# Routed attention and a bilinear FFN on one core: pair numbers instead of counts, closer issues, two more probability rooms

## The chip, the cores and the metric

The kernel runs on one core of one Trainium2 chip. The metric is the device time of one execution in microseconds (us); the table below gives the runs of the kernel before. The profile is of one further execution, recorded with its engines: TensorE (PE, with its weight loads PEld), VectorE (DVE), ScalarE (ACT), GpSimd (POOL) and SyncE (SP), which issues most DMAs.

## What is computed

Queries and keys of each head are assigned to the nearest of 16 centroids; a query attends to the keys of its own cluster alone. The heads' outputs, side by side, are the input of a feed-forward network with two factors. The shapes are (4, 8, 768, 64) for q, k and v, (8, 16, 64) for the centroids, (512, 1536) twice and (1536, 512) for the weights.

```python
q_assign = argmax(q_n @ c_n.T); k_assign = argmax(k_n @ c_n.T)
mask = q_assign[:, :, :, None] == k_assign[:, :, None, :]
scores = where(mask, (q @ k.T) / 8, -1e9)
attn = softmax(scores)
x = (attn @ v).transpose(0, 2, 1, 3).reshape(3072, 512)
out = ((x @ w_a) * (x @ w_b)) @ w_out
```

Inputs, products and output are in 32-bit floats, the one-hot rows in 16-bit ones. The weights come in as 64-bit numbers and are rounded on the chip.

## The kernel before, in words

**Pairs.** Two heads of one batch make a pair; there are 16, 4 of each batch. The first 6 (`ND`) are done densely, the other 10 are sorted by cluster first.

**Dense stage.** A dense pair has 12 units: 2 halves of 384 queries times 6 blocks of 128 keys, 384 columns for each of the two heads. The loop over `g` takes two units per turn. `score` (L587) adds a product of one-hot rows, which puts other clusters far down, and the product of q and k in PSUM; ACT makes the exponentials `pt` (L600) in SBUF; `weigh` (L629) multiplies them by v into `O`; `add_up` (L618) lets DVE add the units of a half up, from which `denominators` (L649) makes the sums over keys. `normalize` (L669 to L682) inverts and applies them on DVE. The buffers for `pt` are 4, so an exponential of unit u waits until unit u-4 was added up and weighed. While a pair is worked on, the next is prepared: `prep_transpose`, or for pairs 4 and 5 DVE transposes (L514), then similarities to the centroids (`prep_sim`, L405), the maximum, the one-hot rows and their way across (`prep_onehot`, or for pairs 4 and 5 small DMAs from `move_one_hot`, L496).

**Sorted pairs.** `sorted_pair` makes a chain of steps per pair: loads of rows (`load_rows` L1308, later `load_blocks`, `load_queries`, `load_keys`), transposes on PE (`across`, L1351, copied by ACT at L1356) or on DVE, similarities (L1362), one-hot rows, counts ahead of each row by matmuls (`prefix`, L1399 and L1401, copied by ACT at L1407), then `index()` on DVE: `totals`, the rank of each cluster by size, `bases`, and the place of each row in a list of 2560 slots (`places`, L1448 and L1453). 24 indirect DMAs per pair (`put`, L1504) scatter rows of q into a DRAM list `qd` and rows of k and v, side by side, into a list `kvd`. `reload` (L1534, L1538) reads the lists back, strip by strip; DVE turns them (L1547), `scores` (L1576), exponentials (L1587) and `values` (L1601, L1610) do attention inside the clusters, `keep` stores the result, 12 indirect DMAs (`get`, L1641) gather it back and `x_across` (L1656) puts it into `xT`. There are 5 (`RING`) lists of each kind; before a list is first used, `clear` (L1277) fills it with zeros.

**Which slots are filled.** A slot that no row was put into must not count. After the places are known, four more steps in `index()` (`overflow`, two comparisons over 512 columns at L1489 and L1493, and the reduction `in_order` at L1467) make a table `cnt` of how many rows each strip of slots holds; `filled` (L1552, L1556) compares it with the place of a slot and writes 1 or 0 into column 64 of the reloaded v, and `only_filled` multiplies v by it. That column also gives the denominators.

**FFN.** Pieces of a deque `ffn` fill PE's time: `up` products of a batch into `h`, then `down` products. The products run as two halves of 64 columns (`in_halves`, L722). Before that, `round_w` rounds a block of 128x512 weights on DVE (L311 to L329) and ACT (L325, L326) after its load (L300). Once the FFN has begun, two PSUM banks of `ps_m` belong to it, and all small products beside it share the third (`beside`).

**What sets the order.** The order on each engine is written by hand and by a planner that runs while the kernel is built: it keeps an assumed clock (`now`, `clocks`), takes the steps of the chains from a heap of due times when their engine's assumed backlog allows, and `spend`s assumed times. The gaps in `plan` (for instance 0.4 ahead of `similarities`, 0.8 ahead of `scores`) are in its time. `paced` sets the issue of each indirect DMA: it takes the next matmul in a list of `marks` (assumed time, instruction) that lies at least `SPACE` behind the one before, and makes the DMA wait for that matmul.

## Time and profile before

| | us |
|---|---|
| median of 3 runs | 968.73 |
| lowest, highest | 965.47, 969.1 |
| the profiled execution | 965.66 |
| its span, from the first to the last instruction | 963.9 |

| engine | busy us | share | instructions |
|---|---|---|---|
| PE | 933.9 | 97% | 8068 |
| DVE | 612.0 | 63% | 1309 |
| POOL | 369.7 | 38% | 373 |
| ACT | 261.4 | 27% | 564 |

In the rows of the profile, a line begins with its place in the kernel (L722) and its engine; `out<-in` are the tiles that it writes and reads. A timeline's row has the start and the duration in us, and in brackets how long the engine sat idle before it and what ended that. A group's row has the count, the busy time in us, the mean duration in ns, and behind a bar the idle time in us. A letter q behind the engine's name (SPq) means its queue, which issues and waits. The DMA share is that of the 16 DMA engines.

### The profile page before, as it was taken

Reading aid. Unit: us, or ns where it says so; the run is one execution under the profiler, and the core shown is the slowest. Engines: PE = TensorE matmul, PEld = TensorE weight load, DVE = VectorE, ACT = ScalarE, POOL = GpSimd, SP = SyncE. Lnnn points to the kernel's source line nnn. Section 1 sums busy time; section 2 is a strip of 40 time slices with the busy share of each in tenths; the row PEclk is TensorE's granted clock in tenths of the full one; section 3 lists DMA queues with packets and bytes.
Section 4 is the critical chain, followed back from the end, with each engine's and each line's share of the span. In section 5 each row is a group of like instructions: output and inputs, shape, how many; then the busy total and the mean of one; then the engine's idle time right before and its main releaser. Section 6 shows DMA issues by size and latency. Waiting matters only on the chain.

```text
span 963.9 us, 20921 instructions
## 1 busy us (share of the span) xinstructions
PE 933.9 (97%) x8068; PEld 495.1 (51%) x8068; DVE 612.0 (63%) x1309; ACT 261.4 (27%) x564; POOL 369.7 (38%) x373
## 2 busy tenths in 40 slices
PE   8999979899999999999999999999999999999997
PEld 5444434344455467645454666545455664444564
DVE  5798887796989795667666746573434343343542
ACT  5775644542343301022221200212221001111100
POOL 1035645465545565555555455455553100000000
PEclk9999999999999999999999999999999999999999
DMA  7967694447799947583867375753734112121310
GB/s 196 232 176 192 146 242 120 148 133 196 182 237 178 207 143 167 118 195 92 178 131 167 112 174 132 161 139 97 151 86 135 34 43 74 56 66 55 116 34 31
DMA packets 309195, 131.82 MB, mean 137 GB/s; under 512 B 230112, under 2 KB 294112, under 8 KB 309088
## 3 DMA queue, kind: packets, MB, share of 16 engines
q1 hardware_dynamic: 297152, 114.23, 49.1%
q0 software_dynamic: 11520, 15.75, 6.0%
q8 instruction: 66, 1.08, 0.5%
q10 hardware_dynamic: 416, 0.43, 0.1%
q14 instruction: 41, 0.34, 0.1%
HBM read 86.93 MB, written 43.20 MB: 135 GB/s over the span
## 4 chain that ended last, share of the span: by engine, by line
PE 91%; DVE 5%; ACT 2%; issue 1%; DMA 1%; DVEq 0%; ACTq 0%
PE m L722 69%; PE s L587 5%; PE O L629 4%; PE s L1576 3%; PE s L1601 2%; PE s L1610 2%; DVE acc L618 1%; PE m L649 1%; PE s L1656 1%; PE O L1362 1%; PE m L1351 1%; ACT pt L600 1%; PE m L405 1%; DMA raw<-in_moe_w_a_dram 0%; DMA h<-in_q_dram 0%
## 5 line engine op out<-in xcount | busy, mean ns | idle before, releaser
L1641 POOL DMA_INDIRECT xT<-od,idx x120 | 119.6, 996 | 114.2 <-PE m L722 72.3
L722 PE MATMUL m<-xT,wa_sb 128*64 128x384 f32 x672 | 118.4, 493 | 0.0
L722 PE MATMUL m<-xT,wb_sb 128*64 128x384 f32 x672 | 116.4, 488 | 2.0 <-issue 1.5
L897 DVE TENSOR_TENSOR ha<-ha,m 128x384 f32<-128x384 f32 x72 | 39.7, 551 | 79.2 <-PE m L722 52.7
L722 PE MATMUL m<-wo_sb,h 128*64 128x256 f32 x768 | 86.9, 380 | 0.0
L894 ACT COPY h<-m 128x384 f32<-128x384 f32 x72 | 34.4, 478 | 179.9 <-PE m L722 153.1
L897 DVE TENSOR_TENSOR h<-h,m 128x384 f32<-128x384 f32 x72 | 39.6, 550 | 68.5 <-PE m L722 46.4
L1504 POOL DMA_INDIRECT kvd<-whole,idx x60 | 60.7, 1012 | 54.6 <-PE m L722 34.3
L1504 POOL DMA_INDIRECT qd<-whole,idx x60 | 59.8, 997 | 53.8 <-PE m L722 36.9
L722 PE MATMUL m<-raw 128*64 128x384 f32 x432 | 79.4, 487 | 0.5 <-ACT h L894 0.5
L722 PEld LDWEIGHTS m<-xT,wb_sb 128*64 128x64 f32 x672 | 47.4, 137 | 61.8 <-issue 58.2
L722 PEld LDWEIGHTS m<-xT,wa_sb 128*64 128x64 f32 x672 | 48.8, 138 | 58.1 <-issue 54.8
L600 ACT ACTIVATE pt<-s 128x768 f32<-128x768 f32 x72 | 55.5, 809 | 51.9 <-PE s L587 32.5
L722 PEld LDWEIGHTS m<-wo_sb,h 128*64 128x64 f32 x768 | 54.7, 137 | 27.9 <-issue 1.1
L722 PE MATMUL m<-xT,h 128*64 128x256 f32 x576 | 64.9, 379 | 0.0
L587 PE MATMUL s<-qkT 64*128 64x384 f32 x288 | 55.1, 503 | 0.0
L1504 POOL DMA_INDIRECT qd<-wo_sb,idx x24 | 25.7, 1070 | 75.6 <-DVE acc L618 59.3
L629 PE MATMUL O<-pt,v 128*64 128x384 f32 x288 | 54.4, 500 | 0.0
L722 PE MATMUL m<-xT,size 128*64 128x384 f32 x288 | 52.7, 487 | 0.0
L1504 POOL DMA_INDIRECT kvd<-h,idx x36 | 39.5, 1097 | 33.8 <-PE m L722 13.7
L722 PEld LDWEIGHTS m<-xT,h 128*64 128x64 f32 x576 | 41.5, 137 | 20.6 <-issue 0.2
L722 PEld LDWEIGHTS m<-raw 128*64 128x64 f32 x432 | 30.7, 137 | 39.2 <-issue 37.3
(262 smaller groups left out, 1490.8 us busy)
## 6 DMA issues: line engine op xcount, KB each, us to landing
whole<-kvd SPq DMA_DIRECT2D x80, 160.0 KB
kvd<-wo_sb SPq DMA_DIRECT2D x25, 256.0 KB
whole<-qd SPq DMA_DIRECT2D x40, 160.0 KB
od<-whole SPq DMA_DIRECT2D x40, 160.0 KB
raw<-in_moe_w_a_dram SPq DMA_DIRECT2D x12, 512.0 KB
raw<-in_moe_w_b_dram SPq DMA_DIRECT2D x12, 512.0 KB
raw<-in_moe_w_out_dram SPq DMA_DIRECT2D x12, 512.0 KB
raw<-up_sums SPq DMA_DIRECT2D x96, 64.0 KB
```

What stands on the lines that cost most here:

```text
L405: nc.tensor.matmul(out=ps[32 * kq:32 * kq + 32, 0:HB], lhsT=cTb[:, hp, :], rhs=qkTs[p][:, kq * HB:(kq + 1) * HB], start=True, stop=True)
L587: ins = nc.tensor.matmul(out=s[:, a, 0:HB], lhsT=Ts[p][r, S + j * P:S + (j + 1) * P], rhs=Ts[p][r, hf * HB:(hf + 1) * HB], start=start, st ...
L600: Sl.activation(out=pt, in_=s[:, :, 0:HB], func=AF.Exp, scale=SCALE)
L629: ins = nc.tensor.matmul(out=O_of[0][a * D:(a + 1) * D, 0:HB], lhsT=vs[p][:, a, j, :], rhs=probs[u][:, a, :], start=(j == 0), stop=(j == N ...
L722: ins = nc.tensor.matmul(out=ps[half], lhsT=lhsT[:, half], rhs=rhs, **kw)
L894: S_.copy(out=box[name], in_=box["X"][:, 0:HB])
L897: V.tensor_tensor(out=box[name], in0=box[name], in1=box[bank][:, 0:HB], op=ALU.add)
L1504: ins = Gi.indirect_dma_start(out=dst[:, :], out_offset=bass.IndirectOffsetOnAxis(ap=M["idx"][:, w, j, a:a + 1], axis=0), in_=src, in_offs ...
L1576: noted(nc.tensor.matmul(out=tiles[s // 2][r0:r0 + m, s % 2, c0:c0 + m], lhsT=M["skT"][r, h, 32 * x:32 * x + m], rhs=M["sqT"][r, h, 32 * x ...
L1601: noted(nc.tensor.matmul(out=ps[:, s, 65 * i:65 * i + 65], lhsT=pt[:, P * i:P * i + P], rhs=vt[:, i, :], start=True, stop=True))
L1610: noted(nc.tensor.matmul(out=ps[r, s, 65 * (2 + i):65 * (3 + i)], lhsT=pt[r, 2 * P + D * i:2 * P + D * i + D], rhs=vt[r, 2 + i, :], start= ...
L1641: paced(Gi.indirect_dma_start(out=M["xs"][:, j, a * D:(a + 1) * D], out_offset=None, in_=od[n][:, :], in_offset=bass.IndirectOffsetOnAxis( ...
```

## The change

The table of counts goes. A row of k and v in `kvd` is one float longer (`KV` = 129): `places` fills that column of the rows in SBUF with the number n of the sorted pair (a memset of 12 columns on DVE), `put` scatters it with the row, `reload` reads it back as column 64 of v, and `filled` is one comparison with n. An old pair's number or a cleared slot differs from n. The constants `place` and `order_of` and the three steps of the table go. The rows of `kvd` are now 516 bytes apart in DRAM.

`SPACE` is 1.62 instead of 1.8, `paced` takes the first mark that is not before the slot, and both halves of a product are in `marks` instead of the second one alone.

`prob_room` gives exponentials 6 rooms instead of 4: two of six lie in the third and fourth quarter of `xTs[1]`, which nothing else uses in the dense stage.

Two gaps of the planner grow: ahead of `similarities` from 0.4 to 1.2, ahead of `scores` from 0.8 to 1.8. The buffer `h` that serves as room for early sorted pairs grows with the longer rows.

```diff
-    SPACE, EARLY, RING = 1.8, 5, 5
+    SPACE, EARLY, RING = 1.62, 5, 5
...
+    def prob_room(u):
+        if u % 6 < 4:
+            return ptp.tile([P, 2, HB], FP32, name="pt")
+        return xTs[1][:, u % 6 - 2].rearrange("p (a t) -> p a t", a=2)
...
-                pt = ptp.tile([P, 2, HB], FP32, name="pt")
+                pt = prob_room(u)
...
             ins = nc.tensor.matmul(out=ps[half], lhsT=lhsT[:, half], rhs=rhs,
                                    **kw)
-        fresh.append(ins.ins.name)
+            fresh.append(ins.ins.name)
...
-    ROWS = 1280
-    kvd = [dram.tile([2 * ROWS + 32, 2 * D], FP32, name=f"kvd{n}") for n in range(RING)]
+    ROWS, KV = 1280, 2 * D + 1
+    kvd = [dram.tile([2 * ROWS + 32, KV], FP32, name=f"kvd{n}") for n in range(RING)]
...
-            t, x = (kvd[n % RING], 20) if i < 5 else (qd[n % RING], 10)
+            t, x, w = (kvd[n % RING], 20, KV) if i < 5 else (qd[n % RING], 10, 2 * D)
...
-                in_=zrow[:, None, :].broadcast_to((P, m, 2 * D)))
+                in_=zrow[:, None, 0:w].broadcast_to((P, m, w)))
...
-        slot = max(issued[0], now[0] - 2.7)
-        t, name = next((x for x in marks if x[0] >= slot - 0.35), marks[-1])
-        issued[0] = max(slot, t - 0.4) + SPACE
+        slot = max(issued[0], now[0] - 3.05)
+        t, name = next((x for x in marks if x[0] >= slot), marks[-1])
+        issued[0] = max(slot, t) + SPACE
...
-                Vs.tensor_copy(out=keys, in_=total[:, 1])
...
+                Vs.memset(M["kvr"][:, :, :, 2 * D], float(n))
...
-            def in_order():
-                M["cnt"] = counts.tile([P, E], FP32, name="cnt_s")
-                Vm.tensor_reduce(out=M["cnt"],
-                                  in_=cmp.rearrange("p a c d -> p (a c) d"),
-                                  axis=AX.X, op=ALU.add)
                 mark("after", n)
...
-                lambda: Vm.tensor_tensor(
-                    out=cmp, in0=halves(rank_of)[:, :, None, :].broadcast_to(shape),
-                    in1=order_of[:, None, :, None].broadcast_to(shape),
-                    op=ALU.is_equal),
-                lambda: Vm.tensor_tensor(
-                    out=cmp, in0=cmp,
-                    in1=halves(keys)[:, :, None, :].broadcast_to(shape), op=ALU.mult),
-                in_order,
...
-                               (M["kvr"][:, a, j], kvd[ring], 2 * D))[w]
+                               (M["kvr"][:, a, j], kvd[ring], KV))[w]
...
-                        out=M["v"][:, s, :, 0:D],
-                        in_=kvd[ring][strip(s), D:2 * D].rearrange(
+                        out=M["v"][:, s],
+                        in_=kvd[ring][strip(s), D:KV].rearrange(
...
+            Vs.tensor_scalar(out=one_, in0=one_, scalar1=float(n), scalar2=None,
+                              op0=ALU.is_equal)
...
-        chain += [plan(FREE, 0.4, similarities, lambda: was("after", n - 1), "T")]
+        chain += [plan(FREE, 1.2, similarities, lambda: was("after", n - 1), "T")]
...
-        chain += [plan(FREE, 0.8, scores, lambda: "T" not in busy, "T"),
+        chain += [plan(FREE, 1.8, scores, lambda: "T" not in busy, "T"),
```

More of the change, by code (lines that the diff above doesn't have):

```diff
@@ L192, in short_path @@
     lists = pool("lists", 9)
-    counts = pool("counts", 5)
     xtp = pool("xtp", 2)
@@ L771, in piece_a @@
                 run_due()
-            box["h"] = early[blk].rearrange("p (f t) -> p f t", f=NF)
+            box["h"] = early[blk][:, 0:NF * HB].rearrange("p (f t) -> p f t", f=NF)
             ps = up(wa_sb, f)
@@ L1137, in short_path @@
     oh = zero.tile([P, 2, NJ + 1, 2 * NC], BF16, name="oh_s")
-    place = zero.tile([P, 2], FP32, name="place")
-    order_of = zero.tile([P, NC], FP32, name="order_of")
     for b in range(2):
@@ L1142, in short_path @@
     extra = xTs[1].rearrange("p c s -> p (c s)")
-    zrow = wo_sb.rearrange("p f n -> p (f n)")[:, NF * DM - 2 * D:]
+    zrow = wo_sb.rearrange("p f n -> p (f n)")[:, NF * DM - KV:]
     R_ = {}
@@ L1148, in short_path @@
     wanted, issued = {}, [0.0]
-    ROW = 2 * NJ * 3 * D
+    ROW = 2 * NJ * (D + KV)
     def rooms(rows, qkT, temp, kk):
@@ L1154, in rooms @@
         R_["kk"] = kk[:, 0:2 * NJ * D].rearrange("p (j a d) -> p j a d", a=2, j=NJ)
-        R_["blocks"] = [t[:, 2 * NJ * D:ROW] for t in rows]
+        R_["blocks"] = [t[:, 2 * NJ * D:2 * NJ * D + 2 * S] for t in rows]
         R_["kvr"] = [t[:, 2 * NJ * D:ROW].rearrange("p (a j d) -> p a j d", a=2, j=NJ)
@@ L1172, in sorted_constants @@
         V.memset(oh, 0.0)
-        ints = extra[:, P:P + 32].bitcast(INT32)
-        nc.gpsimd.iota(ints[:, 0:NC], pattern=[[1, 2], [2, NC // 2]], base=0,
-                       channel_multiplier=0)
-        nc.gpsimd.iota(ints[:, NC:NC + 1], pattern=[[0, 1]], base=0,
-                       channel_multiplier=1)
-        V.tensor_copy(out=order_of, in_=ints[:, 0:NC])
-        V.tensor_copy(out=place[:, 0:1], in_=ints[:, NC:NC + 1])
-        Vs.tensor_copy(out=place[0:D, 1:2], in_=place[0:D, 0:1])
-        V.tensor_scalar(out=place[D:P, 1:2], in0=place[D:P, 0:1],
-                                scalar1=-float(D), scalar2=None, op0=ALU.add)
     def early_room():
-        t = hp_.tile([P, NF * HB], FP32, name="h")
+        t = hp_.tile([P, 2 * ROW], FP32, name="h")
         early.append(t)
@@ L1305, in load_rows @@
             some = (((q, qr[:, :, a]), (k, kk[:, :, a])),
-                    ((k, kvr[:, a, :, 0:D]), (v, kvr[:, a, :, D:])))[second]
+                    ((k, kvr[:, a, :, 0:D]), (v, kvr[:, a, :, D:2 * D])))[second]
             for src, to in some:
@@ L1414, in index @@
             rnk, u, h2 = (x.bitcast(INT32) for x in room_[5:8])
-            sums, keys = room_[8][:, 0:G], room_[9]
+            sums = room_[8][:, 0:G]
             halves = lambda x: x.rearrange("p (a c) -> p a c", a=2)
@@ L1549, in filled @@
         def filled():
-            cnt = M["cnt"].rearrange("p (s h) -> p s h", s=4)
             one_ = M["v"][:, :, :, D]
-            Vs.tensor_scalar(out=one_[:, :, 0:2], in0=cnt[:, :, 0:2],
-                              scalar1=place[:, 0:1], scalar2=None, op0=ALU.is_gt)
-            for hh in range(2):
-                r = slice(D * hh, D * hh + D)
-                Vs.tensor_scalar(
-                    out=one_[r, :, 2:5],
-                    in0=cnt[r, :, 2:8].rearrange("p s (i e) -> p s i e", e=2)[
-                        :, :, :, hh],
-                    scalar1=place[r, 1:2], scalar2=None, op0=ALU.is_gt)
+            Vs.tensor_scalar(out=one_, in0=one_, scalar1=float(n), scalar2=None,
+                              op0=ALU.is_equal)
         def only_filled(g):
@@ L1702, in sorted_pair @@
         chain += row(FREE, 0.3, later("find", 7), "V")
-        chain += [plan(FREE, 0, lambda: run_chain(row(FREE, 0.2, later("after", 4), "B"), 0.0, start, n))]
+        chain += [plan(FREE, 0, lambda: run_chain(row(FREE, 0.2, later("after", 1), "B"), 0.0, start, n))]
         chain += row(-12, 0.3, [lambda wja=wja: put(*wja) for wja in order], "G",
```

## The prediction

> **What bounds the kernel now.** I read the page first, then the busy time in windows of 20 us, then the timelines of the engines around every hole on TensorE.

> ```profile
> span 963.9 us, 20921 instructions
> ...
> PE 933.9 (97%) x8068; PEld 495.1 (51%) x8068; DVE 612.0 (63%) x1309; ACT 261.4 (27%) x564; POOL 369.7 (38%) x373
> ```

> TensorE is busy for 933.9 of 963.9 us, so at most 30 us can be won by taking waits away, plus what a lowered clock costs. The changed kernel issues as many matmuls as the old one (9138 in both built programs), so the question is only which holes go and which come. The windows (columns: us, busy us and count of PE, PEld, DVE, ACT and POOL, granted clock, DMA share, GB/s) say where they are:

> ```profile
> 80.00:100.00 20.00, 17.99 (x113) 8.18 (x113) 19.10 (x43) 12.12 (x23) 11.16 (x11) 0.91 0.56 147
> ...
> 120.00:140.00 20.00, 14.79 (x80) 5.98 (x78) 17.98 (x37) 8.95 (x17) 8.29 (x9) 0.91 1.02 271
> ...
> 800.00:820.00 20.00, 20.00 (x128) 8.90 (x124) 7.25 (x14) 3.82 (x8) 0.00 (x0) 1.00 0.23 64
> ```

> Late stages are full; the holes are in the dense stage, where DVE is at 18 to 19 of 20 us. From 230 us on only one group of holes is left, inside the sorted score products, without a releaser:

> ```profile
> PE s L1576 <- issue: 4.1, 12, 0.4
> ```

> The timeline of PE (start, us, what, in brackets the idle time before it and its releaser) gives the holes that the sum goes by:

> ```profile
> 90.06 0.50 PE L587 MATMUL s<-ohT 64*128 64x384 bf16 x2 [2.01 <-ACT pt L600]
> 90.33 2.79 PE L587 MATMUL s<-qkT 64*128 64x384 f32 x8
> ...
> 94.91 1.45 PE L587 MATMUL s<-qkT 64*128 64x384 f32 x8
> ...
> 102.19 0.85 PE L405 MATMUL m<-qkT,cTb 128*32 128x384 f32 x8
> ...
> 123.38 0.34 PE L587 MATMUL s<-ohT 64*128 64x384 bf16 x2 [2.92 <-DMA wo_sb<-in_q_dram]
> ...
> 133.12 1.70 PE L405 MATMUL m<-qkT,cTb 128*32 128x384 f32 x8 [1.24 <-DVE qkT L514]
> ...
> 139.40 0.87 PE L649 MATMUL m<-pt,ones 128*64 128x384 f32 x4 [0.68 <-ACT wo_sb L1356]
> ...
> 159.57 0.87 PE L649 MATMUL m<-pt,ones 128*64 128x384 f32 x4 [1.62 <-ACT wo_sb L1407]
> ...
> 177.93 0.66 PE L1351 MATMUL m<-ident,wo_sb 128*128 128x128 f32 x4 [3.60 <-ACT wo_sb L1356]
> 178.51 4.49 PE L722 MATMUL m<-xT,wa_sb 128*64 128x384 f32 x16
> ...
> 191.24 2.75 PE L722 MATMUL m<-xT,wb_sb 128*64 128x384 f32 x16
> ...
> 214.28 2.80 PE L722 MATMUL m<-xT,wb_sb 128*64 128x384 f32 x16 [1.49 <-issue]
> ```

> Call them A (2.01 us), B (2.92), C (1.24), D (0.68), E (1.62), F (3.60) and G (1.49). After A the same eight score products took 2.79 instead of 1.45 us, 1.34 more; after F the block of 16 took 4.49 instead of 2.75, 1.74 more. The reason is the granted clock:

> ```profile
> 90.00:93.00 3.00, 2.94 (x10) 0.50 0.30 72
> ```

> In this trace the waits of 2.01 us and more (A, B, F) cost half a clock behind them, those of 1.62 and less (C, D, E, G) did not. [...]

> What stands behind A, B and F is seen on ACT, which works in order:

> ```profile
> 89.20 0.81 ACT L600 ACTIVATE pt<-s 128x768 f32<-128x768 f32 x1 [4.34 <-DVE acc L618]
> ...
> 121.12 0.67 ACT L325 ACTIVATE size<-raw 128x512 f32<-128x512 f32 x1 [1.79 <-DMA raw<-in_moe_w_a_dram]
> ...
> 176.59 0.81 ACT L600 ACTIVATE pt<-s 128x768 f32<-128x768 f32 x1 [3.27 <-DVE acc L618]
> ```

> At A and F an exponential waited 4.34 and 3.27 us for DVE's running sum to free its probability buffer. At B it was not the buffer: the rounding of a weight block, ahead of the exponential on ACT, waited for its load.

> **The change part by part.** *Two more rooms.* The exponentials of group g wait for the sums of group g-3 instead of g-2: one more group of slack. That covers A and, with the copy of transposed rows that stood behind the exponential, F. B stays.

> *Counts go.* Per sorted pair DVE loses one copy, two 512-column operations and one reduction, and gains one memset of 12 columns (after the rows: groups of DVE from 60 to 221 us, with count, busy us, mean ns):

> ```profile
> L1493 DVE TENSOR_TENSOR wo_sb<-wo_sb 128x512 f32<-128x512 f32 x5 | 3.4, 687 | 0.1
> L1489 DVE TENSOR_TENSOR wo_sb<-wo_sb,order_of 128x512 f32<-128x512 f32 x5 | 3.4, 683 | 0.0
> ...
> L1484 DVE TENSOR_TENSOR wo_sb<-wo_sb,oh_s 128x384 f32<-128x384 f32 x5 | 2.8, 559 | 0.2
> L1481 DVE TENSOR_TENSOR wo_sb<-wo_sb 128x384 f32<-128x384 f32 x5 | 2.8, 558 | 0.1
> L1448 DVE TENSOR_REDUCE wo_sb<-wo_sb 128x24 f32<-128x384 f32 x5 | 2.8, 552 | 0.1
> L1467 DVE TENSOR_REDUCE cnt_s<-wo_sb 128x32 f32<-128x512 f32 x4 | 2.7, 676 | 0.1
> ...
> L1453 DVE TENSOR_SCALAR idx<-wo_sb 128x24 int32<-128x24 f32 x5 | 1.2, 249 | 0.2
> ...
> L1426 DVE COPY wo_sb<-wo_sb 128x32 f32<-128x32 f32 x4 | 0.7, 171 | 0.0
> ```

> The memset isn't in the trace; its nearest row is the 32-column copy (0.17 us), its upper end the index cast (0.25); I take 0.2. So 0.69+0.68+0.68+0.17-0.2 = 2.0 us less per pair. It also adds a wait on DVE for the loads of k and v and for the puts out of the same room. Queued behind it are running sums, for which exponentials and so PE wait. For pair 2 the last load was issued here,

> ```profile
> 55.48 1.17 SPq L1308 DMA_DIRECT2D h<-in_v_dram  x1
> ```

> and its index list was written 34 us later;

> ```profile
> 89.58 0.31 DVE L1453 TENSOR_SCALAR idx<-wo_sb 128x24 int32<-128x24 f32 x1
> ```

> With that cover I cost the wait at nothing, and at the load's lateness if that cover goes. The lighter marking of filled slots (three operations to one) falls in the stage after 220 us, where PE waits for no DVE: nothing.

> *Stage of A.* PE gains 2.01+1.34 = 3.35 us and reaches the similarity products of dense pair 4 (L405, 102.19) at 98.84. They need DVE's transposes, before which DVE worked without a break:

> ```profile
> 99.14 1.83 DVE L514 STREAM_TRANSPOSE qkT<-qk 128x768 f32<-128x768 f32 x2
> ```

> They end at 100.97, less what is removed before them (0.17+0.68+0.69-0.2 = 1.34): 99.63. So 0.8 of the 3.35 comes back as a wait at L405; 2.5 is left. This is the next in line once A goes.

> *Stage of B.* Nothing in the built order moves the load ahead: it still stands behind the eight moves of the one-hot rows on SP. It and PE come 2.5 sooner alike: B stays whole.

> *Stage of C.* The built order has, ahead of dense pair 5's transposes, the three index operations, the index cast and the memset of sorted pair 3, which stood behind them: 0.56+0.56+0.55+0.25+0.2-0.17 = 1.95 us later on DVE. On PE two groups of row transposes (0.66 each, the row at 177.93) now come before the similarity products. The wait is then 1.24+1.95-1.3 = 1.9 us; against before, the stage keeps 2.5-1.95+1.3 = 1.85.

> *Stages of D, E, F.* Transposes, counts of slots and denominators share one PSUM bank there, so each must wait until ACT has copied the one before. The new order puts FFN work between them at D and E, and the rooms remove F: 0.68+1.62+3.60+1.74 = 7.64 go. But for sorted pair 5 denominators now follow directly behind the second group of row transposes, and again behind the prefix sums, each time with the copy behind an FFN copy and a rounding on ACT: the situation of E, which I price at E's 1.62 twice (bounds: D's 0.68 and F's 3.60). 4.4 is left.

> *G* is FFN waiting for a rounding that DVE had not come to. In the built order two more roundings stand ahead of the last running sums: 1.49 goes.

> *1.62 apart.* POOL's issues come closer and bind to the first half product too. PE waits for POOL nowhere, so the result is only where the sorted work falls in PE's order: the last transposition back stands 12 matmuls earlier of 3549, and FFN fills the rest. Nothing; a loss up to the size of a late hole (0.4) per pair, a gain up to the 4.1 us of L1576. The wider gaps before similarities and scores go the same way.

> *Rows of 516 bytes.* POOL's time per put does not go by width:

> ```profile
> L1504 POOL DMA_INDIRECT kvd<-whole,idx x60 | 60.7, 1012 | 54.6 <-PE m L722 34.3
> ...
> L1504 POOL DMA_INDIRECT qd<-whole,idx x60 | 59.8, 997 | 53.8 <-PE m L722 36.9
> ```

> (512 against 256 bytes.) Reloads have cover: the last is issued at 685.1, DVE's last turn of such rows starts at 696.9, and no turn waited for a load:

> ```profile
> L1538 SPq DMA_DIRECT2D whole<-kvd x40: 373/576/1398, 226.0 to 685.1; - x40
> ```
> ```profile
> L1547 DVE STREAM_TRANSPOSE whole<-whole x40: 794/837/846, 239.1 to 696.9; 128x640 f32<-128x640 f32 x40
> ```

> Cost nothing, if the clears do not hold up the weight loads (third rival).

> **Sum.** 1.85+4.4+1.49 = 7.7 us. Of the three new waits (1.9, 1.62, 1.62) the first is nearest to A: one half-clock stretch, 1.34. Left: 6.4. The profiled execution took 965.66 us, so 959.3. The three runs lie at 965.47, 968.73 and 969.1; the profiled one is 3.07 under their median. I do not know which level the next runs take, and add half of that: 960.8.

> **Rivals.**
> 1. *Waits of another name* (20%): all three new waits cost a half-clock stretch of 1.74. Speaks for it: 1.9 and 1.62 lie against A's 2.01; against it: C and E. 965.66-7.7+5.2 = 963.2, with the half level 964.7: no change that a measurement tells.
> 2. *A free DVE* (12%): the slack carries through, B and the wait at C vanish too: 7.7+1.9+2.92+1.34 = 13.9, so 951.8, or 953.3. Against it: B's releaser is a load.
> 3. *Slower: late weight loads* (18%). The clears write rows that are 4 bytes longer and lie off the old pitch; DMA is full from 120 to 140 us (share 1.02, 271 GB/s).

> ```profile
> kvd<-wo_sb SPq DMA_DIRECT2D x25, 256.0 KB
> ```

> 25 of them are 6.4 MB, 23.6 us at 271 GB/s. If they took half as long again, 11.8 us more of a full DMA, 0.47 each with one or two ahead of a weight load. B shows that a rounding without slack holds the exponentials: 2.92+1.34 = 4.26 each. From three such roundings on it loses: 959.3+12.8 = 972.1, or 973.6. The built order also puts one weight load behind eight row loads instead of four. Against it: B was the only such wait among the roundings of the stage. [...]
> 4. *The rooms are not what holds* (10%): ACT's order holds the exponentials anyway, A and F stay. 7.7-2.5-5.34 = -0.1: 965.8, or 967.3. Against it: the 4.34 and 3.27 us put down to DVE.

> **Numbers.** The forecast has 40%, 957 to 963. Within 0.5% of 968.73 is 4.8 us, about what a measurement tells from no change; faster begins under 963.9. Faster: forecast 36, rival 2 12, of rival 1 2, together 0.50. Same: 4 of the forecast, 18 of rival 1, rival 4: 0.32. Slower: rival 3, 0.18. The range takes in the forecast, rivals 1 and 4 and nearly all of 2, not all of 3: 951 to 970.

> **What would show it.** After: no exponential waits for L618; granted clock 1.00 around 90 us; a wait of 0.8 before L405 near 100 and 1.9 near 131; B's wait still there; two waits before L649 near 175 and 195 released by ACT's copies; none where G was; POOL's last put earlier with PE full behind it. I am wrong if the holes of the dense stage still add up to what they were, if roundings wait for loads more than once, or if holes open after 230 us.

## The result, and the profile after

| | median us | lowest, highest | runs |
|---|---|---|---|
| before | 967.37 | 962.51, 974.03 | 14 |
| after | 976.96 | 971.92, 981.17 | 14 |

The changed kernel is slower: the ratio is 1.0092, with a 95% interval of 1.0070 to 1.0115. The forecast was 960.8 us and faster, the range ended at 970. The profiled execution took 977.24 us. From the page after:

```profile
span 975.5 us, 20900 instructions
...
PE 935.9 (96%) x8068; PEld 496.8 (51%) x8068; DVE 589.1 (60%) x1255; ACT 260.8 (27%) x564; POOL 366.4 (38%) x371
```

DVE lost 22.9 us of work as meant, and TensorE was still idle 9.6 us longer. The windows after (columns as before) say where. The first three answer to those shown before, the last three hold the stages:

```profile
80.00:100.00 20.00, 18.34 (x126) 8.54 (x126) 19.01 (x43) 12.64 (x24) 13.15 (x12) 1.00 0.92 196
120.00:140.00 20.00, 10.46 (x56) 4.36 (x52) 17.11 (x36) 10.13 (x20) 6.92 (x7) 0.83 1.12 257
800.00:820.00 20.00, 20.00 (x146) 10.18 (x144) 8.61 (x17) 2.87 (x6) 0.00 (x0) 1.00 0.26 78
...
35.00:220.00 185.00, 169.00 (x1127) 76.26 (x1127) 152.75 (x300) 103.06 (x210) 88.49 (x84) 0.97 0.78 178
220.00:500.00 280.00, 271.84 (x2757) 149.48 (x2755) 191.99 (x423) 68.15 (x160) 147.80 (x146) 1.00 0.75 162
500.00:840.00 340.00, 333.51 (x3006) 183.23 (x3004) 169.68 (x365) 52.30 (x122) 127.38 (x130) 1.00 0.50 114
```

Before, the last three held 169.91, 275.97 and 338.62 us of PE. So the dense stage did not gain, and the two late ones lost 4.1 and 5.1 us. At 80 to 100 us the clock stays whole, as forecast; at 120 to 140 PE fell from 14.79 to 10.46 us. PE's timeline there and later has, in brackets, the waits that stand where A, B and C stood (first fence) and the two that were forecast before the denominators (second fence):

```profile
94.03 0.34 PE L591 MATMUL s<-ohT 64*128 64x384 bf16 x2 [1.30 <-issue]
...
126.54 0.50 PE L591 MATMUL s<-ohT 64*128 64x384 bf16 x2 [6.15 <-ACT xT L604]
139.21 2.19 PE L404 MATMUL m<-qkT,cTb 128*32 128x384 f32 x8 [3.20 <-DVE qkT L513]
```
```profile
182.83 0.87 PE L653 MATMUL m<-xT,ones 128*64 128x384 f32 x4 [1.87 <-issue]
...
202.93 0.87 PE L653 MATMUL m<-xT,ones 128*64 128x384 f32 x4 [1.54 <-ACT wo_sb L1399]
```

B grew from 2.92 to 6.15 us, and C from 1.24 to 3.20. The stage of A gained nothing: PE reaches the similarity products of dense pair 4 at 102.18 us, where it reached them at 102.19. ACT's timeline shows what holds the exponential at B:

```profile
121.97 0.67 ACT L324 ACTIVATE size<-raw 128x512 f32<-128x512 f32 x1 [6.92 <-DMA raw<-in_moe_w_a_dram]
...
123.86 0.65 ACT L324 ACTIVATE size<-raw 128x512 f32<-128x512 f32 x1
...
125.26 0.51 ACT L1399 COPY wo_sb<-m 128x448 f32<-128x448 f32 x1
125.68 1.51 ACT L604 ACTIVATE xT<-s 128x768 f32<-128x768 f32 x2
```

Two roundings of weights stand ahead of it. Before, round 7 (a block of `w_b` that had long landed) came first and was done while round 8's load was under way; the exponential followed round 8 alone. Now round 8 comes first, and round 7 and a copy wait behind it although their data is there. SP's timeline has both loads:

```profile
106.30 0.68 SPq L299 DMA_DIRECT2D raw<-in_moe_w_b_dram  x1
...
112.34 5.36 SPq L495 DMA_DIRECT2D ohT<-h  x8
117.80 0.53 SPq L299 DMA_DIRECT2D raw<-in_moe_w_a_dram  x1
```

The load itself stands where it stood; the order of what waits for it changed. Round 7 is due at a fixed turn of the loop over `g`, round 8 as soon as its load counts as arrived and the planner's clock shows DVE idle (`may_round`: `clocks["V"] <= now[0] + 0.6`). With less DVE work booked it shows that earlier, and round 8 overtakes.

From 225 to 850 us PE waited for these, from the table of waits after (us in total, times, longest):

```profile
PE s L1546 <- issue: 4.6, 12, 0.5
PE m L726 <- issue: 2.3, 5, 0.9
PE m L726 <- ACT rest L1046: 2.2, 1, 2.2
PE m L726 <- DMA comb<-up_sums: 2.1, 1, 2.1
PE m L726 <- DMA raw<-up_sums: 1.1, 1, 1.1
PE m L726 <- DVE raw L863: 1.0, 1, 1.0
PE m L726 <- DVE h L783: 1.0, 1, 1.0
```

Before, the first row (4.1) and one of 0.5 were all. The rest is new: ten waits of FFN products, each at another place. SP's timeline at the one for `comb`:

```profile
681.99 0.96 SPq L860 DMA_DIRECT2D size<-up_sums  x2
683.13 1.98 SPq L1512 DMA_DIRECT2D whole<-qd  x4
685.45 3.11 SPq L1512 DMA_DIRECT2D whole<-kvd  x4
688.60 3.99 SPq L1516 DMA_DIRECT2D whole<-kvd  x4
692.70 1.33 SPq L860 DMA_DIRECT2D raw<-up_sums  x2
694.22 0.76 SPq L860 DMA_DIRECT2D comb<-up_sums  x2
```

Twelve reloads of a sorted pair (9.1 us of SP) stand ahead of sums that FFN needs at 695.5. That could be slow transfers or a bad order; the page can't tell.

### The profile page after: what moved, and what is told of

It reads as the page before. It is cut to its first block, busy times and chain, and to the rows that moved or that the text cites. A ratio compares the mean times of both kernels' runs of the same rounds, so it can differ in the third digit from the quotient of the medians.

```text
span 975.5 us, 20900 instructions
## 1 busy us (share of the span) xinstructions
PE 935.9 (96%) x8068; PEld 496.8 (51%) x8068; DVE 589.1 (60%) x1255; ACT 260.8 (27%) x564; POOL 366.4 (38%) x371
## 2 busy tenths in 40 slices
DMA packets 309195, 132.04 MB, mean 135 GB/s; under 512 B 230112, under 2 KB 294112, under 8 KB 309088
## 3 DMA queue, kind: packets, MB, share of 16 engines
q1 hardware_dynamic: 297152, 114.38, 52.5%
## 4 chain that ended last, share of the span: by engine, by line
PE 85%; issue 4%; DVE 4%; DMA 2%; SPq 2%; ACT 1%; POOL 1%; DVEq 0%; POOLq 0%; ACTq 0%
PE m L726 64%; PE s L591 5%; PE O L633 4%; PE s L1546 3%; PE s L1571 2%; PE s L1580 2%; PE m L653 1%; PE s L1626 1%; PE m L404 1%; PE m L388 1%; PE O L1354 1%; SPq L1512 1%; PE m L1343 1%; SPq L495 0%; DVE acc L622 0%
## 5 line engine op out<-in xcount | busy, mean ns | idle before, releaser
L901 DVE TENSOR_TENSOR h<-h,m 128x384 f32<-128x384 f32 x72 | 39.7, 553 | 79.7 <-PE m L726 54.6
L1482 POOL DMA_INDIRECT qd<-wo_sb,idx x24 | 24.5, 1019 | 76.4 <-DMA kvd<-wo_sb 60.7
L1482 POOL DMA_INDIRECT qd<-h,idx x36 | 37.7, 1047 | 37.5 <-PE s L591 14.9
L898 ACT COPY ha<-m 128x384 f32<-128x384 f32 x54 | 25.9, 479 | 86.4 <-PE m L726 75.1
L1482 POOL DMA_INDIRECT kvd<-h,idx x36 | 37.5, 1042 | 29.5 <-PE m L726 7.5
```

The costliest lines, as they stand in the source:

```text
L898: S_.copy(out=box[name], in_=box["X"][:, 0:HB])
L901: V.tensor_tensor(out=box[name], in0=box[name], in1=box[bank][:, 0:HB], op=ALU.add)
L1482: ins = Gi.indirect_dma_start(out=dst[:, :], out_offset=bass.IndirectOffsetOnAxis(ap=M["idx"][:, w, j, a:a + 1], axis=0), in_=src, in_offs ...
```

## The experiments

Ratios are to the kernel before on the same chip, with the 95% interval. Most of these chips run the kernel before in 953 to 954 us, the one of the page before in 967.37; where a single wait is compared with that page, it is a comparison across chips. The theories: **R**, rows of 516 bytes are slow; **P**, closer issues crowd the transfers; **W**, the operations of the pair numbers themselves cost it; **O**, the order that the planner makes costs it.

**Single parts.** Each is the kernel before with one part of the change (the parts are the paragraphs of "The change"; the rest of its diff is left out).

x_numbers: 

> The change's first part alone: pair numbers in 516-byte rows in place of counts; rooms for probabilities, pace and gaps as before. Theory O: the planner, with less DVE work to place, rounds the wa block of round 8 ahead of round 7's; that wait of 6.15 us in place of 2.92, and a late stage with about 10 more us of PE gaps if its reloads stand together: ratio 1.006 to 1.013. Theory R: the same late loss but no part of it from the order, 1.005 to 1.010. Theory P (the pace of the issues costs it): 0.997 to 1.002, since the pace is that of before.

x_pace: 

> The change's second part alone: scattered rows issued 1.62 apart and bound to half products; counts, rows of 512 bytes, rooms and gaps as before. Theory P (denser issues crowd the transfers of the late stage): 1.004 to 1.010, with the late stage's PE gaps several us above the 4.8 us of before. Theories O and R: within 0.997 to 1.002, since the order of the weight roundings stays that of before.

x_rooms: 

> The change's third part alone: six rooms for probabilities in place of four; all else as before. All theories: the exponential no longer waits for the product before last in the dense stage, the gaps D, E and F go, and one or two of 1.62 us come before the denominators: a gain of 3 to 6 us, ratio 0.994 to 0.997, with the late stage as before. If the rooms are not what holds, 0.999 to 1.001.

x_gaps: 

> The change's last part alone: the two gaps in the chain of a pair (ahead of the similarities 1.2 in place of 0.4, ahead of the scores 1.8 in place of 0.8), all else as before. If the gaps take back the rooms' gain (0.9938 to 0.9987 in the run without pair numbers): 1.002 to 1.006, with waits at the gate of the FFN products between 290 and 400 us that the kernel before does not have. If not: 0.998 to 1.002.

| part | ratio | interval |
|---|---|---|
| pair numbers (x_numbers) | 1.0115 | 1.0098 to 1.0132 |
| pace (x_pace) | 1.0014 | 1.0005 to 1.0024 |
| rooms (x_rooms) | 0.9938 | 0.9921 to 0.9955 |
| two gaps (x_gaps) | 1.0074 | 1.0045 to 1.0103 |

The pace is nearly free: P falls. The rooms bring 5.4 us of medians (953.91 to 948.56). Pair numbers and, unexpectedly, the gaps lose. The product of the four is 1.0141, above the 1.0092 of all together by a little more than the intervals allow, so they do not simply multiply.

**The width alone.** x_rows516 scatters rows of 129 floats whose last one nobody uses; TensorE, ScalarE and SyncE issue exactly in the order of before.

```diff
-    kvd = [dram.tile([2 * ROWS + 32, 2 * D], FP32, name=f"kvd{n}") for n in range(RING)]
+    kvd = [dram.tile([2 * ROWS + 32, KV], FP32, name=f"kvd{n}") for n in range(RING)]
```

> The kernel before, with its counts, its order of instructions and its pace, but each scattered row of k and v is 129 numbers wide in the scratch tile (516 bytes, the last number is not used), and the clears write rows of that width. Only widths differ, and five small memsets of the unused column are added. Theory R (rows off the pitch of 512 bytes cost the time): 972 to 977 us, a ratio of 1.005 to 1.010, with the late stage's waits for the comb copies and the sums' loads grown as they grew in the changed kernel, by some 5 to 9 us. Theory O (the planner's order costs it, not the width of the rows): 0.999 to 1.002, and the late stage's PE gaps within 1.5 us of those before (4.8 us), however much longer one packet takes.

Measured: 1.0017 (1.0005 to 1.0028). The transfers did get slower. The pages of before and of this run, the queue's share of 16 engines' time:

```profile
q1 hardware_dynamic: 297152, 114.23, 49.1%
```
```profile
q1 hardware_dynamic: 297152, 114.28, 54.4%
```

As many packets took 54.4% instead of 49.1%, but no wait above 0.15 us came on PE after 225 us. One wait grew: B is 4.20 us here, as ACT's rounding waits 3.51 us for the load of its block (1.79 before). In the order of before, R explains 0.17%, not 0.92%.

**The order kept, the operations gone.** An operation's time is booked when its name is looked up in the planner's wrapper of the engine. x_numbers_booked looks up the removed operations without calling them:

```diff
+            def in_order():
+                Vm.tensor_reduce
                 mark("after", n)
...
                 overflow,
+                lambda: Vm.tensor_tensor,
+                lambda: Vm.tensor_tensor,
+                in_order,
```

> Pair numbers in 516-byte rows as in the run of the first part alone, but the removed VectorE operations stay booked in the planner's clock without being issued (three of the count, one copy, two of the filling, four of the setup; the new memset is not booked). TensorE, ScalarE and SyncE then issue exactly what the kernel before issues, in its order; only VectorE has less to do and rows are wider. Theory O (the order that the planner makes from a freer VectorE costs the time): 0.999 to 1.003, of which 1.0017 is the measured price of the wide rows, and no wait of over 4.5 us at the exponential near 120. Theory W (the operations or the data of the pair numbers cost it: the new column's write, its return in the reload, the one comparison): 1.008 to 1.012, as the part alone measured (1.0115).

Measured: 1.0008 (0.9998 to 1.0018). TensorE, ScalarE and SyncE issue in the order of before, and the loss is gone. The table of PE's waits from 225 to 850 us, first in x_numbers, then in x_numbers_booked, which is this one row:

```profile
PE m L726 <- DMA raw<-up_sums: 2.0, 2, 1.4
PE m L726 <- DVE raw L863: 1.7, 1, 1.7
PE m L726 <- DVE h L1013: 1.5, 2, 1.3
PE m L726 <- DVE ha L901: 1.0, 1, 1.0
PE m L726 <- DMA xT<-down_sums: 1.0, 1, 1.0
PE m L726 <- DVE h L783: 0.8, 1, 0.8
```
```profile
PE m L726 <- DMA raw<-up_sums: 0.2, 1, 0.2
```

The wait of 1.7 shows what such an order is. DVE's timeline of x_numbers has four transposes of a sorted pair ahead of the sums for which the FFN product waits until 409.59:

```profile
405.69 3.17 DVE L1525 STREAM_TRANSPOSE whole<-whole 128x640 f32<-128x640 f32 x4
408.79 0.45 DVE L863 TENSOR_TENSOR comb<-wa_sb 128x128 f32<-128x128 f32 x2
409.15 0.49 DVE L863 TENSOR_TENSOR raw<-comb,wa_sb 128x128 f32<-128x128 f32 x2
```

**The operations kept, the order changed.** x_counts_unbooked is the reverse: the counts are issued through `nc.vector`, past the planner's clock.

```diff
-                Vs.tensor_copy(out=keys, in_=total[:, 1])
+                nc.vector.tensor_copy(out=keys, in_=total[:, 1])
```

> The kernel before, with its counts and its rows of 512 bytes, and every VectorE operation issued that it issued; but the operations that the pair numbers replace are no longer booked in the planner's clock (and one small one is booked in place of the memset). TensorE, ScalarE and SyncE then issue in the order of the run of pair numbers alone, while VectorE works as much as before. Theory O (the order alone): 1.008 to 1.013, since it measured 1.0115 with the wide rows and a freer VectorE. Theory W (order matters only together with the wide rows): 1.000 to 1.005.

Measured: 1.0071 (1.0048 to 1.0094), a little under the range of O, with B at 4.83 us. Nothing of the change is in this kernel but the order. O is shown as a cost of its own, and W can't be the whole: its range ended at 1.005, where the interval begins (1.0048). What lies between 1.0071 and 1.0115 is not split further. B takes two parts: the swap with narrow rows makes it 4.83 us, the wide rows without the swap 4.20; added to the 2.92 of before, the two growths (1.91 and 1.28) come to 6.11, against 6.15 in the changed kernel.

**The swapped rounding alone.** One condition in `next_round` keeps the rounds in turn, in the part alone (x_numbers_in_order) and in the changed kernel (x_after_in_order):

```diff
-        if not (i in raws and arrived[i] + (4.5 if i < 22 else 3.5) <= now[0] and may_round(i)):
+        if not (i in raws and min(raws) == i and arrived[i] + (4.5 if i < 22 else 3.5) <= now[0] and may_round(i)):
```

> Pair numbers alone with one condition more in the planner: a round of weights is rounded only if no earlier round waits, so that round 7 goes ahead of round 8 again; the rest of the order stays that of the freer VectorE. Theory O-early (the swap of the two roundings is most of the loss): 1.000 to 1.005. Theory O-late (most of it is the order of the loads and stores after 250 us): 1.007 to 1.010, with the wait near 120 back at 2.5 to 4.2 us and the late gaps of 8 to 10 us as in the part alone.

> The changed kernel with the one condition that a round of weights is rounded only if no earlier round waits. In the part alone this condition took 1.0115 to 1.0088. If the swapped rounding (wait of 6.15 us near 120) is a term of its own in the changed kernel too: 1.005 to 1.008, with that wait back under 4.6 us; the late stage keeps its gaps. If the swap only stands for a loss that another wait takes over: 1.008 to 1.011.

Measured: 1.0088 (1.0070 to 1.0106) and 1.0066 (1.0049 to 1.0083), so about 0.26% or 2.5 us by either (the intervals overlap). PE's row at B in the second one:

```profile
121.00 0.50 PE L591 MATMUL s<-ohT 64*128 64x384 bf16 x2 [4.23 <-ACT xT L604]
```

The swap is a term of its own, but the smaller one. In both kernels the waits of FFN products after 225 us stay.

**The other parts together, and the change with its bookings kept.** x_no_numbers joins rooms, pace and gaps to the kernel before; x_after_booked is the changed kernel with the bookings of x_numbers_booked.

> The changed kernel with the first part undone: counts by slot and rows of 512 bytes as before; six rooms, the pace of 1.62 and the two gaps of the change. All forms of theory O, and theory W: the parts without pair numbers bring 0.994 to 0.998. If parts work against each other in some way that single edits do not show (the two gaps, which move the chain of each pair), 1.000 to 1.006.

> The changed kernel with the same ten VectorE operations booked in the planner and not issued. Theory O: 0.994 to 0.998, the sum of six rooms (0.9938), pace (1.0014) and wide rows (1.0017) and of two gaps not measured yet; faster than the kernel before. Theory W: 1.005 to 1.010, as the changed kernel itself (1.0092).

Measured: 0.9987 (0.9975 to 0.9999) and 1.0029 (1.0015 to 1.0042). Both are short of what was expected: even with the old bookings, the changed kernel does not win. The two issue in the same order on TensorE, ScalarE and SyncE, so here the pair numbers and their wide rows cost 0.4% with the order kept, where they cost 0.08% in the order of before. W and R are thus not nothing in every order. B is 4.51 us instead of 2.66; where the rest lies is open, as the profiled execution of x_after_booked was its fastest (953.47 us, median 956.19). In ratios the changed kernel's loss then parts into -0.1% (other parts), 0.4% (pair numbers in the order kept) and 0.6% (the order without the bookings).

Rooms and pace without the gaps tell why the other parts bring so little:

> Six rooms and the pace of 1.62 bound to half products; counts and gaps as before. If the pace takes back the rooms' gain: 0.997 to 1.000. If the gaps do: 0.994 to 0.996, the product of rooms and pace measured singly (0.9938 and 1.0014).

Measured: 0.9960 (0.9947 to 0.9973). So of the rooms' gain the pace takes some 0.2% (its interval touches that of the rooms alone), and the gaps 0.3% more. PE's rows with waits over 1 us after 225 us in x_gaps (before had none) are again FFN products behind DVE:

```profile
299.39 2.80 PE L722 MATMUL m<-xT,wa_sb 128*64 128x384 f32 x16 [1.43 <-DVE h L779]
402.15 1.51 PE L722 MATMUL m<-raw 128*64 128x384 f32 x8 [1.11 <-DVE raw L859]
```

With three smaller ones they make 4.1 us; the rest of the 0.74% (7 us) is not placed.

**How much does any other order cost?** Three kernels change one constant of the planner and not one instruction.

```diff
-                                 for us in (0.56, 0.19, 0.29, 0.44, 0.7, 0.83, 0.96))
+                                 for us in (0.56, 0.18, 0.29, 0.44, 0.7, 0.83, 0.96))
```

x_vs_plus: 

> The kernel before with one constant of the planner changed: each short VectorE operation is booked at 0.20 us in place of 0.19. No instruction is added or taken away; only the order changes. Theory F (a freer VectorE is what makes the planner's order bad): no loss here, 0.998 to 1.003, since it books more, not less. Theory S (the order is so sensitive that any small change of what is booked gives another, and the one of before is a good one by choice): 1.003 to 1.012.

x_vs_minus: 

> The same with 0.18 us in place of 0.19. Theory F: 1.000 to 1.004 (a small step towards the freer VectorE, about a fifth of what the pair numbers free). Theory S: 1.003 to 1.012, on the same side as the step to 0.20.

x_vm_plus: 

> The kernel before with the middle VectorE operations booked at 0.71 us in place of 0.70; again only the order changes. Theory F: 0.998 to 1.003. Theory S: 1.003 to 1.012.

Measured: 0.9988 (0.9971 to 1.0005), 0.9967 (0.9953 to 0.9980), 1.0024 (1.0004 to 1.0043). A step of 0.01 us changes over a thousand places in PE's order, and the time by up to 0.3% to either side. S as it was put (always slower) falls. F does not hold either: booking less (0.18) gained where F put no change or a loss. The two that book more lie in F's ranges.

**Which booking?** x_only_count_booked books only the three operations of the count.

> Pair numbers alone, with only the three removed operations of the count booked in the planner (2.1 us of booked time per pair) and the copy, the filling and the setup left out of its clock; the memset is booked. The roundings then keep their order. If the booked time of the count is what moves the order to the bad one: 1.000 to 1.004. If any of the removed bookings does (the late order is bad with each of them): 1.006 to 1.010.

Measured: 1.0051 (1.0035 to 1.0068), between both. B is 2.03 us there, and others come in its place, 2.75 us before an FFN product near 330 among them. So the bookings of the count, given back, take away about half of the loss; which of the other bookings makes the rest was not tried. Why the orders made with fewer bookings (1.0051 to 1.0115) all lie at the bad end, when 0.18 did not, stays open.

**Rooms with something else.** x_rooms_numbers_booked joins six rooms and pair numbers in the order of the rooms alone; x_rooms_vs_minus joins six rooms and the 0.18.

> Six rooms and pair numbers, with the removed VectorE operations booked in the planner; pace and gaps as before. TensorE, ScalarE and SyncE issue in the order of the run of the rooms alone. If the costs add: 0.9938 by the rooms plus 0.0008 by the pair numbers in the same order, 0.993 to 0.997, faster than both kernels. If the rooms' gain needs the narrower rows (the load ahead of the exponential near 120 comes later): 0.998 to 1.002.

> Six rooms, and short VectorE operations booked at 0.18 us in place of 0.19; counts, pace and gaps as before. If the two gains add (0.9938 and 0.9967): 0.989 to 0.992, the fastest here. If the order of 0.18 us gained by the same waits that the rooms take away: 0.993 to 0.997.

Measured: 0.9951 (0.9934 to 0.9967) and 0.9931 (0.9914 to 0.9947). Both beat both kernels, neither is told apart from the rooms alone (0.9938). In none of the three orders that were kept did pair numbers bring anything: the DVE work they save was on no path.

## Why the prediction was wrong

**The step that failed is "Nothing in the built order moves the load ahead ... B stays whole", and with it the "Nothing" for the late stages.** I looked for a changed place of the load and found none, which is right. What changed is the place of a rounding whose data had landed: round 7 fell behind round 8 on ACT and DVE. B became 6.15 us instead of 2.92; keeping the turn gives 2.5 us back. The rest of B's growth is the load: its rounding starts 1.58 us after PE's last product ends, instead of 0.66, and x_rows516 shows such a delay from wide rows alone. I had even quoted ACT's rounding that waits at B.

**The terms put at nothing after 220 us: "where PE waits for no DVE: nothing", and "Nothing" for issues 1.62 apart and the wider gaps.** This was true of the order of before. I treated that order as given and costed the operations; the planner lays it anew. The late waits of FFN products rose from 0.5 to 9.7 us (2.2+2.1+1.1+1.0+1.0 with a releaser, 2.3 without). I had bounded a loss at a late hole of 0.4 per pair; single holes of 1 to 2.2 came. The profiled execution came 17.9 us above the 959.3 of the sum: 9.2 us of PE's work are missing from the two late windows, and in the dense stage 0.9 us were lost where 6.4 were to be won. The closer issues were nearly free (1.0014), as put; the gaps, which I set down with them, were not (1.0074).

**Two more rooms: right in mechanism.** Alone they bring 5.4 us; in x_rooms PE has no wait at A, 0.23 us at F, and 0.21 of the forecast 0.8 before the similarity products. That is less than the 2.5 and 5.34 put on A and F, and on another chip: with the order of before, A is only 0.60 us there (x_rows516), without a half clock behind it (granted clock from 35 to 220 us 0.98, before 0.97). In the changed kernel the 2.5 did not come at all. A was replaced by 1.30 and 0.36, the copies of one-hot rows being ahead of the exponential on ACT, which I had not in the sum; 0.67 came at 75.81; and PE was 1.2 us late from 37 us on (1.1 in x_rooms too; the cause is open). The wait of 0.8 did not come, since PE came no earlier.

**The new waits before the denominators: right.** 1.62 twice was forecast, 1.87 and 1.54 came, and G went.

**C: right in kind, short in size.** 1.9 forecast, 3.20 came, and a stretch of half clock behind it (the eight products at L404 took 2.19 us instead of 1.70).

**The clock.** Besides B's stretch of half clock I forecast one more, 1.34. B's longer wait took two (123.2 to 130.0), and C's one (140.3 to 143.7): 10.2 us at half clock in all, as much as in the three stretches of before (the one at the end of the execution is left out).

**Rows of 516 bytes: nearly right in the order of before, not in that of the change.** 0.17% instead of nothing there; 0.4% together with the pair numbers in the order of x_no_numbers. Rival 3 had the right sign, and its mechanism at one place, not at three: B is 2.71 us in x_rooms and 4.44 in x_rooms_numbers_booked, which has the same order with wide rows. Clears that take half as long again were an assumption that no run shows; measured is the queue's share over all its transfers, 49.1 to 54.4% in x_rows516. That decided little here, since most transfers had cover (no wait above 0.15 us on PE after 225 us); the load at B had none (ACT waits 3.51 us for it, 1.79 before). None of the four rivals was the planner's order. Two of the signs that I had named for being wrong came, though: the holes of the dense stage added up to what they were, and holes opened after 230 us.

## What to carry over

Where a program lays out the order from booked times, an edit has two prices: that of its operations, and that of the order that its bookings make. Part them by booking what is gone without issuing it, and by issuing it without booking; if only one of the two kernels is slow, retune the order before judging the edit. Test in more than one order: pair numbers cost 0.08% in one and 0.4% in another. Before crediting an engine's saved work, ask whether anything waits for it: here 22.9 us less DVE brought nothing. And a forecast from the old trace should give the order itself a price, here 0.3% to either side for a step of 0.01 us.

## What the runs showed of the hardware

**The lowered clock does not go by a wait's length alone.** My reading of before (2.01 us and more cost half a clock, 1.62 and less don't) does not hold. With six rooms, the wait near 120 is 2.71 us in x_rooms and 2.62 in x_rooms_vs_minus. Their windows:

```profile
120.00:130.00 10.00, 8.21 (x40) 3.11 (x39) 9.48 (x23) 5.84 (x11) 3.82 (x4) 0.83 1.11 258
```
```profile
120.00:130.00 10.00, 7.54 (x46) 3.17 (x47) 9.48 (x23) 5.14 (x10) 3.05 (x4) 1.00 1.09 262
```

The first lost half a clock for about 3.4 of the ten us (0.83), the second nothing (1.00). In the changed kernel waits of 2.23 us (an FFN product at 376.07, behind ACT) and of 2.07 (the one for `comb`, at 697.56) cost nothing either: the clock is 1.00 from 372 to 380 and from 694 to 702 us.

**Longer packets were nearly free here.** In the order of before, a tenth more time (49.1 to 54.4%) of the queue that carries most transfers (297152 of 309195 packets) cost 0.17%. It showed where a load had no cover: B, 4.20 us instead of 2.92.
